# Sliding-window attention and an expert layer on one core: values' products with the exponentials as weights, tokens on partitions

## The chip, the cores and the metric

The kernel runs on one core of a Trainium2 chip. The metric is the device time of one execution in microseconds (us). A NeuronCore has a matrix engine (PE, TensorE), a vector engine (DVE), a scalar engine (ACT), a general engine (POOL, GpSimd) and a queue engine that issues transfers (SP). Matrix products are written to PSUM, eight banks of 512 f32 columns on 128 partitions; DVE and ACT copy them to SBUF.

## What is computed

Eight batches with eight heads of 576 tokens and 64 channels go through attention in which a token sees itself and the 127 tokens before it, with a slope by head. The result, 4608 tokens of 512 channels, goes to a layer of eight experts: each token to the expert with the highest logit.

```
scores = q k^T / 8;  mask = (0 <= i - j < 128)
attn = softmax(where(mask, scores - slope[h] * |i - j|, -1e9));  x = attn v     # then (B*S, H*D) = (4608, 512)
logits = x w_gate;  e = argmax(logits);  g = softmax(logits)[e]
y = g * (relu(x w1[e]) w2[e])
```

## The kernel before

**Attention.** The work is cut into 16 units: four pairs of batches (`bp`) times four pairs of heads (`hp`, 128 channels). In a unit, `c` is the batch of the pair and `r` the head of the pair. Keys are cut into nine blocks `kb` of 64 tokens; a block of keys meets at most 192 queries. Four groups `g` of a unit hold the key blocks (0,1), (2,3), (4,5), (6,7,8). `scores(i)` makes the scores of group `i` with keys on partitions (L739), one exponential over both heads (ACT, L745) and one multiplication by a table of slopes and mask (DVE, L748 or L753). The result `pe` has keys on partitions (batch `c` on its half) and queries along the free dimension. Scores run two groups ahead (`AHEAD = 2`).

`values(u, half, kbs)` has `v` (64 keys x 64 channels) as weights and `pe` (64 keys x up to 192 queries) as the moving operand. Its result has channels on partitions and queries along the free dimension, in the two banks of `at` (pool `ps_a`, one buffer of two banks), once for queries 0 to 319 and once for 320 to 575. `finish` copies `at` to `xT` (ACT, L791 and L793) and makes the sums of the exponentials with a second set of products (L806): an indicator `ind` as weights, `pe` as the moving operand once more, into a bank `m` of pool `ps_m` (two buffers); DVE adds them to `sumT` (L817), ACT copies the first (L815).

**Routing.** When a pair of batches is through, `behind(bp)` gives a list of tasks, of which `some()` runs one entry after each group: `gate` (three products of `xT` with the gate's weights, L826), `turn` (transposes of the logits and sums so that tokens are on partitions, L850), `scale_a` to `scale_c` (reciprocals of the sums, logits, softmax, on DVE), `count`, `place`, `ones_at`, `enlist` (each token's slot at its expert), and nine rows: `row_turned` transposes 128 tokens of `xT` (L984) and copies them (ACT, L986), `row_out` adds the scales (POOL, L990) and writes the row tile to `x_d` (SP, L992). After the third pair of batches the list is dense (ten entries) and ends with a gather (L1090, POOL) of the first expert's tokens. The last pair's tasks run inside the first expert group (`with_tail`).

**Experts.** For each expert four tiles of 128 tokens are gathered, scaled (L501), transposed (L1107), and multiplied in a Strassen form (L1273, L1330), with single tiles (L1369, L1385) for what exceeds 512 tokens. This part begins at 195.16 us and fills the rest.

**Order.** All of it has a manual schedule: an engine runs its instructions in the order in which the program emits them, and waits where an operand or a buffer is late. On PE the order in a step is scores of two groups on, values of this group, then one entry of tasks. On ACT the exponential of two groups on stands ahead of the copies of this group, and on DVE its multiplication does. SP issues the loads of `q`, `k` and half of `v` two units ahead (three buffers each), the row tiles and the expert weights; POOL the other half of `v`, and the gathers.

An f32 matrix product is two passes on PE, each with its own weight load; a transpose is one. With weights of 64 rows and 64 columns four products lie at four places of the array: rows by `c`, columns by `r`.

## Time and profile before

Times of three runs: 717.45, 714.87 and 713.62 us, median 714.87. The profiled execution took 721.67 us, its span is 719.9 us, the mean granted PE clock 0.987.

| what | value |
| --- | --- |
| busy share of the span | PE 95%, DVE 48%, ACT 31%, POOL 18% |
| attention and most of routing | to 195.16 us, where the first expert product starts |
| first expert group with the last pair's routing | 195.16 us to 259.73 us, where the second one's products start |
| first exponential of units 3, 7 and 11 | 37.28, 75.86 and 120.21 us |
| products of values, of sums, of scores (instructions, passes) | 1408, 704, 1152 |
| bytes moved | 122.00 MB, mean 169 GB/s |

A busy share of PE is of little use as a bound, since ends of matrix instructions are modelled and overlap. What one step costs is read from the starts of successive groups in the timeline.

### The profile page before, as it was taken

How to read it: one execution, taken by the hardware profiler on the slowest of the kernel's cores; microseconds unless marked ns; L12 is line 12 of the kernel's file. 1: busy time of each engine (PE TensorE's matmuls, PEld its weight loads, DVE VectorE, ACT ScalarE, POOL GpSimd, SP SyncE). 2: the span in 40 equal slices, each digit the busy share in tenths (PEclk: the TensorE clock that was granted, in tenths of full speed). 3: DMA queues.
4: the chain of work that ended last, by engine and by line, in shares of the span. 5: the costliest groups of instructions: out<-in, count | busy, mean ns of one | idle time of the engine just before them, and what ended most of it. 6: DMA issues, size and time to landing. Idle time of an engine off the chain costs nothing.

```text
span 719.9 us, 14588 instructions
## 1 busy us (share of the span) xinstructions
PE 683.4 (95%) x6204; PEld 570.3 (79%) x6204; DVE 347.1 (48%) x671; ACT 225.5 (31%) x410; POOL 132.1 (18%) x222
## 2 busy tenths in 40 slices
PE   6799999889899999999999999999999999999995
PEld 5677778667678888878887888788788978878892
DVE  3356738775457675443642545255245534433410
ACT  4455546455334223202311321232133023203200
POOL 4320133310200250023022102301220230021020
PEclk9999999999999999999999999999999999999998
DMA  9977876773424961186328236731843482184010
GB/s 249 241 208 264 235 229 182 194 211 109 126 76 166 354 244 45 74 272 226 117 81 305 111 117 199 293 117 27 287 182 117 164 303 77 64 287 153 1 59 8
DMA packets 52091, 122.00 MB, mean 169 GB/s; under 512 B 3679, under 2 KB 14527, under 8 KB 52016
## 3 DMA queue, kind: packets, MB, share of 16 engines
q1 hardware_dynamic: 43120, 95.66, 40.0%
q0 software_dynamic: 7744, 24.43, 10.2%
q8 instruction: 51, 0.84, 0.5%
q10 hardware_dynamic: 1152, 0.88, 0.4%
q14 instruction: 24, 0.20, 0.1%
HBM read 101.79 MB, written 19.96 MB: 169 GB/s over the span
## 4 chain that ended last, share of the span: by engine, by line
issue 57%; PE 22%; POOL 10%; DVE 4%; ACT 3%; DMA 3%; POOLq 0%; SPq 0%; ACTq 0%; DVEq 0%
PE sp L739 6%; PE at L774 6%; POOL out_dram L1353 5%; POOL xg L1090 5%; PE m L984 2%; PE m L806 2%; DMA q_sb<-in_qT_dram 2%; ACT pe L745 1%; PE m L970 1%; PE pair0b L1273 1%; ACT xT L791 1%; PE m L826 1%; DVE pe L748 1%; DMA out_dram<-zo,s_idx 1%; PE m L850 1%
## 5 line engine op out<-in xcount | busy, mean ns | idle before, releaser
L1353 POOL DMA_INDIRECT out_dram<-zo,s_idx x39 | 43.8, 1123 | 384.2 <-DVE zo L1344 283.4
L748 DVE TENSOR_TENSOR pe<-pe,fac 128x768 f32<-128x768 f32 x48 | 48.3, 1007 | 48.7 <-ACT pe L745 48.6
L774 PE MATMUL at<-pe,v_sb 64*64 64x192 f32 (+2 forms) x1408 | 63.0, 292 | 9.1 <-ACT xT L791 6.5
L739 PE MATMUL sp<-q_sb,k_sb 64*64 64x192 f32 (+2 forms) x1152 | 61.7, 330 | 7.5 <-DMA q_sb<-in_qT_dram 6.5
L745 ACT ACTIVATE pe<-sp 128x768 f32<-128x768 f32 x64 | 51.9, 810 | 51.2 <-PE sp L739 45.5
L774 PEld LDWEIGHTS at<-pe,v_sb 64*64 64x64 f32 x1408 | 48.5, 138 | 15.6 <-ACT xT L791 8.6
L739 PEld LDWEIGHTS sp<-q_sb,k_sb 64*64 64x64 f32 x1152 | 42.8, 141 | 19.8 <-issue 6.4
L1090 POOL DMA_INDIRECT xg<-x_rows,g_idx x39 | 42.7, 1094 | 30.6 <-DVE tb L1013 13.2
L806 PE MATMUL m<-pe,ind 128*32 128x192 f32 (+2 forms) x704 | 30.4, 288 | 5.3 <-issue 4.9
L1108 ACT COPY xgT<-m 128x512 f32<-128x512 f32 x39 | 22.8, 585 | 36.8 <-PE m L1107 35.9
L1284 ACT ACTIVATE h<-h 128x512 f32<-128x512 f32 x32 | 20.2, 630 | 40.3 <-DVE h L1283 35.0
L986 ACT COPY xs<-m 128x512 f32<-128x512 f32 x36 | 20.5, 584 | 33.1 <-PE m L984 23.9
L806 PEld LDWEIGHTS m<-pe,ind 128*32 128x32 f32 x704 | 23.4, 110 | 8.3 <-issue 5.8
L501 DVE TENSOR_TENSOR xn<-xg 128x512 f32<-128x512 f32 x39 | 26.1, 685 | 7.6 <-PE m L1107 6.6
L990 POOL COPY xs<-ext 128x16 f32<-128x16 f32 x36 | 10.5, 303 | 85.7 <-DMA x_rows<-xs 40.1
L608 POOL DMA_DIRECT2D v_sb<-in_v_dram x15 | 11.2, 744 | 77.4 <-PE at L774 75.6
L1107 PE MATMUL m<-ident,xn 128*128 128x128 f32 x156 | 23.6, 274 | 0.7 <-DVE xn L501 0.7
L1107 PEld LDWEIGHTS m<-ident,xn 128*128 128x128 f32 x156 | 19.2, 141 | 4.9 <-PE m L1107 0.9
L984 PE MATMUL m<-ident,xT 128*128 128x128 f32 x144 | 22.5, 289 | 0.5 <-DVE hole L1021 0.5
L1385 PE MATMUL pair2a<-w,h 128*128 128x512 f32 x48 | 21.1, 592 | 0.0
L984 PEld LDWEIGHTS m<-ident,xT 128*128 128x128 f32 x144 | 16.9, 150 | 3.9 <-issue 1.7
L791 ACT COPY xT<-at 128x640 f32<-128x640 f32 (+1 forms) x32 | 18.6, 581 | 2.9 <-PE at L774 2.2
(357 smaller groups left out, 1389.8 us busy)
## 6 DMA issues: line engine op xcount, KB each, us to landing
w<-in_moe_w_dram SPq DMA_DIRECT2D x30, 2048.0 KB, 8.9
k_sb<-in_kT_dram SPq DMA_DIRECT2D x15, 576.0 KB, 6.6
q_sb<-in_qT_dram SPq DMA_DIRECT2D x15, 576.0 KB, 7.4
x_rows<-xs SPq DMA_DIRECT2D x32, 264.0 KB, 2.6
v_sb<-in_v_dram SPq DMA_DIRECT2D x15, 288.0 KB, 6.9
v_sb<-in_v_dram POOLq DMA_DIRECT2D x15, 288.0 KB
x_rows<-xs SPq DMA_DIRECT2D x8, 132.0 KB, 2.4
xg<-x_rows,g_idx POOLq DMA_INDIRECT x39
```

Source lines behind the costliest of these rows:

```text
L501: nc.vector.tensor_tensor(to.rearrange("p (h d) -> p h d", h=H), rows[:, :Dm].rearrange("p (h d) -> p h d", h=H), rows[:, Dm : Dm + H].uns ...
L739: nc.tensor.matmul(sp[c * KB : (c + 1) * KB, r, c0 : c0 + n], lhsT=k_sb[u][hs, c, kb * KB : (kb + 1) * KB], rhs=q_sb[u][hs, c, kb * KB : k ...
L745: nc.scalar.activation(pe[:], sp[:, :, :GC], AF.Exp, scale=SCALE)
L748: nc.vector.tensor_tensor(pe.rearrange("p r (k c) -> p r k c", k=2), pe.rearrange("p r (k c) -> p r k c", k=2), fac[:, h0 : h0 + 2, None, ...
L774: nc.tensor.matmul(acc[r * D : (r + 1) * D, c, lo - q0 : hi - q0], lhsT=v_sb[u][c * KB : (c + 1) * KB, kb, r * D : (r + 1) * D], rhs=pe[c ...
L791: nc.scalar.copy(xT[bp][:, hp, : 2 * LQ].rearrange("p (b q) -> p b q", b=2)[:, :, q0 : q0 + n], acc[:, :, :n])
L806: nc.tensor.matmul(sm[32 * j : 32 * j + 32, lo - q0 : hi - q0], lhsT=none[:] if pe is None else ind[:, hp, :], rhs=fac[:, 0, :KB] if pe is ...
L984: nc.tensor.transpose(ps[:, hp * P : (hp + 1) * P], xT[bp][:, hp, t * P : (t + 1) * P], ident[:])
L1090: nc.gpsimd.indirect_dma_start(out=g["xg"][:, j, :], out_offset=None, in_=src, in_offset=bass.IndirectOffsetOnAxis(ap=g_idx[:, g["c0"] + j ...
L1107: nc.tensor.transpose(tp[:, db * P : (db + 1) * P], xn[:, db * P : (db + 1) * P], ident[:])
L1108: nc.scalar.copy(g["xT"][:, :, j * P : (j + 1) * P], tp.rearrange("p (d q) -> p d q", d=DB))
L1353: ins = nc.gpsimd.indirect_dma_start(out=out[:, :], out_offset=bass.IndirectOffsetOnAxis(ap=s_idx[:, g["c0"] + j : g["c0"] + j + 1], axis= ...
```

## The change

The operands of the values' products change places. `pe` (64 keys x 64 queries) is now the weights, and `v` of one head (64 keys x 64 channels, and beside it a column of ones) the moving operand of 65 columns. The result has tokens on partitions, and the column of ones yields the sum of the exponentials. A tile of `v` has 130 columns: ones, head 0, head 1, ones. Places of the array are by `c` (rows) and by the parity of the query block (columns); a product of which only one parity is there (the first query block's step, the last block) has two places at a time.

- `values(u, g, between)` makes, in group `g`, the two query blocks `2g` and `2g+1` (in the last also block 8), each over up to three key blocks, in two banks out of three (`ps_a` has three single banks; `ps_m` is left with one during attention, and has two after it). ACT copies the bank of `c = 0` into the row tile `R`, DVE that of `c = 1`; in the last group each copies block 8 too.
- The second products (L806), their copies and additions, `finish`, `ind` and `none` are gone.
- `R[bp]` holds nine tiles of 128 tokens as they go to `x_d` (520 columns instead of 528). `to_gate` transposes a tile of `R` for the gate (nine times for a pair of batches), into `xT` of two tiles. `gate` is made five times with up to 256 tokens, copied by ACT. `turn` is made five times with two tiles; DVE takes the reciprocal of the sums and multiplies straight out of PSUM.
- `row_turned` and `row_out` are gone. `scale_c` writes the scales into the columns of sums in `R`, and `rows_out` writes the tiles in three calls (two transfers of four tiles and two of 64 rows). `token_scales` reads the new layout.
- `some()` is called at four places of a group: in the middle and at the end of the scores, in the middle and at the end of the values. The lists get more and smaller entries, in those of the first two pairs every second one empty. `within` starts nine transposes and gates in the last unit of the pair itself.
- `ones_at` makes `oc` with two instructions instead of nine; `scale_a` adds heads in three steps instead of one reduction.
- The loads of unit 2 and 3 are emitted somewhat later, in the same order on SP.

```
-                        nc.tensor.matmul(
-                            acc[r * D : (r + 1) * D, c, lo - q0 : hi - q0],
-                            lhsT=v_sb[u][c * KB : (c + 1) * KB, kb, r * D : (r + 1) * D],
-                            rhs=pe[c * KB : (c + 1) * KB, r, c0 + lo - kb * KB : c0 + hi - kb * KB],
+            acc = [ps_a.tile([P, 512], F32, name="at") for c in range(2)]
+            if g:
+                steps = [[(2 * g, 2 * g - 2 + s), (2 * g + 1, 2 * g - 1 + s)] for s in range(3)]
+            else:
+                steps = [[(0, 0), (1, 0)], [(1, 1)]]
...
+                nc.tensor.matmul(
+                    acc[c][j * KB : (j + 1) * KB, x0 + r * (D + 1) : x0 + (r + 1) * (D + 1)],
+                    lhsT=pe[c * KB : (c + 1) * KB, r, k0 : k0 + KB],
+                    rhs=v_sb[u][c * KB : (c + 1) * KB, kb, r * (D + 1) : (r + 1) * (D + 1)],
...
+            for s, step in enumerate(steps):
+                for r in range(2):
+                    for qb, kb in step:
+                        for c in range(2):
+                            product(c, qb % 2, r, qb, kb, 0)
+                if s == 0:
+                    between()
+            if g == 3:
+                for kb in range(NK - 3, NK):
+                    for r in range(2):
+                        for c in range(2):
+                            product(c, c, r, NK - 1, kb, HW)
+            xs = slice(hp * HW, (hp + 1) * HW)
+            for c, copy in enumerate((nc.scalar.copy, nc.vector.tensor_copy)):
+                copy(R[bp][:, 4 * c + g, xs], acc[c][:, :HW])
...
+        def to_gate(bp, k, part):
+            t = slice_of(k)[part]
...
+            ps = m_bank()
+            for hp in range(HP):
+                nc.tensor.transpose(
+                    ps[:, hp * P : (hp + 1) * P], R[bp][:, t, hp * HW + 1 : hp * HW + 1 + P], ident[:],
+                )
+            nc.scalar.copy(xT[bp, k][:, :, part * P : (part + 1) * P], ps.rearrange("p (h q) -> p h q", h=HP))
...
+            todo = [[T(3, 0)], [G(2)], [T(3, 1)], [U(1)], [T(4, 0)], [G(3)], [U(2)], [G(4)], [U(3)], [U(4)], [i], [a],
+                    [b], [n, c], outs[0:1], outs[1:2], outs[2:3], [p], [], [o], [], [e]]
+            return [f for t in todo for f in (t, [])]
...
+            if g == 0:
+                return [T(0, 0), [], T(0, 1), []]
+            if g == 1:
+                return [T(1, 0), G(0), T(1, 1), []]
+            return [T(2, 0), G(1), T(2, 1), U(0)]
```

In the lists T is `to_gate`, G `gate`, U `turn`, i `in_range`, a, b, c the scales, n `count`, p `place`, o `ones_at`, e `enlist`.

## Prediction

> **What bounds the kernel now.** I read the page's groups first, then the chain of waits, the table of windows, and the timeline of single steps.
>
> ```profile
> span 719.9 us, 14588 instructions
> ...
> L748 DVE TENSOR_TENSOR pe<-pe,fac 128x768 f32<-128x768 f32 x48 | 48.3, 1007 | 48.7 <-ACT pe L745 48.6
> L774 PE MATMUL at<-pe,v_sb 64*64 64x192 f32 (+2 forms) x1408 | 63.0, 292 | 9.1 <-ACT xT L791 6.5
> L739 PE MATMUL sp<-q_sb,k_sb 64*64 64x192 f32 (+2 forms) x1152 | 61.7, 330 | 7.5 <-DMA q_sb<-in_qT_dram 6.5
> L745 ACT ACTIVATE pe<-sp 128x768 f32<-128x768 f32 x64 | 51.9, 810 | 51.2 <-PE sp L739 45.5
> ...
> L806 PE MATMUL m<-pe,ind 128*32 128x192 f32 (+2 forms) x704 | 30.4, 288 | 5.3 <-issue 4.9
> ```
>
> ACT and DVE wait for PE (45.5 and 48.6 us of idle time end that way), PE hardly for them: attention is bound by PE, whose stream L806 takes 30.4 us of. The expert part is PE alone and is not changed, so everything is decided before the first expert group's end. Two rows of the chain and three of the timeline give the pace:
>
> ```profile
> 75.86 0.81 ACT pe L745
> ...
> 120.21 0.81 ACT pe L745
> ```
>
> ```profile
> 37.28 0.81 ACT L745 ACTIVATE pe<-sp 128x768 f32<-128x768 f32 x1 [0.39 <-PE sp L739]
> ...
> 38.73 0.89 PE L774 MATMUL at<-pe,v_sb 64*64 64x64 f32 x24 [0.50 <-ACT xT L791]
> ...
> 45.10 0.81 ACT L745 ACTIVATE pe<-sp 128x768 f32<-128x768 f32 x1 [0.39 <-PE sp L739]
> ...
> 195.16 1.89 PE L1273 MATMUL pair0a<-xgT,w 128*128 128x256 f32 x8
> ```
>
> Unit 3, without tasks, takes 45.10 - 37.28 = 7.82 us. Units 3 to 10, with two pairs' routing, take (120.21 - 37.28) / 2 = 41.5 us for four. From 120.21 to the first expert product are 75.0 us.
>
> **What a step costs.** The 24 passes at 38.73 are six steps of four places, of 2 x (64 + 128 + 192) = 768 columns; 0.89 less 0.22 (one pass of 64 columns alone, 229 ns by form) is 0.67 us: 0.87 ns a column, 0.056 us for a step of 64. Rows for the copies and for a task:
>
> ```profile
> 108.82 0.72 PE L774 MATMUL at<-pe,v_sb 64*64 64x192 f32 x16
> ...
> 109.48 0.66 PE L984 MATMUL m<-ident,xT 128*128 128x128 f32 x4
> ...
> 110.06 0.88 PE L739 MATMUL sp<-q_sb,k_sb 64*64 64x192 f32 x16
> ...
> 110.22 0.59 ACT L986 COPY xs<-m 128x512 f32<-128x512 f32 x1 [0.34 <-PE m L984]
> ```
>
> ```profile
> L793 ACT COPY xT<-at 128x128 f32<-128x128 f32 x16 | 4.5, 282 | 0.0
> ...
> L833 DVE TENSOR_TENSOR gs<-m,sumT 128x128 f32<-128x128 f32 x3 | 0.9, 288 | 1.9 <-PE m L826 1.9
> ...
> L975 DVE COPY listed<-m 128x48 f32<-128x48 f32 x1 | 0.2, 209 | 1.7 <-PE m L970 1.7
> ```
>
> **The change, part by part.**
>
> *A unit without tasks.* Scores stay: 3072 columns, 2.6 us. Values: 8, 12, 12 and 24 steps in the four groups (block 8 and half of the first group have two places only), 56 x 0.056 = 3.1 us, against 3072 columns before, 2.6. So the exchange alone costs 0.5 us; what it gains is L806 (1600 columns, 1.4 us, with two changes of array shape) and the wait of 0.50 for `xT`. PE 5.7 us. New waits: three banks hold one and a half groups, and ACT copies its bank only after the exponential that stands before it (0.23 from the end of PE's stream to ACT's start: a pass of 192 columns outlasts its slot by some 0.16, and 0.07 for the signal; then 0.81, the copy 0.28, 0.05 back: 1.37 us after the scores' end). The next group needs that bank after 0.44 to 1.3 us of values and 0.65 of scores: it waits 0.3 us behind the first group, some 0.05 behind two others. In all 6.1 us, 1.7 less than 7.82. ACT needs 4 x 0.81 + 5 x 0.28 = 4.6, DVE 4 x 0.96 + 5 copies. A copy of 130 columns from PSUM isn't there: above 0.21 (48 columns), under 0.48 (128x320 with an addition, L817); I take 0.29, the row of 128 columns. DVE 5.3 us.
>
> *The bank of the tasks.* `ps_m` keeps one bank in attention. A transpose of a tile holds it from 109.48 to 110.22 + 0.59 = 110.81, and 0.05 for the wake-up: 1.38 us. A gate of 256 tokens 0.43 + 0.23 + 0.37 (L815, 256 columns) + 0.05, about 1.0; a turn, with a multiplication of 0.29, 0.8. Nine, five and five are a chain of 12.4 + 5 + 4 = 21.4 us. They stand at almost every second place from the second group of a pair's last unit on, a few tenths of PE work apart, and PE can't pass a waiting task: behind it stand the rest of the scores, and so the next exponential. Exponentials get between these evictions on ACT, by the orders of both engines about every third, and the reciprocals and multiplications of `turn` stand behind a 0.96 us multiplication on DVE twice: +3. So about 24.5 us for two units; of PE work there are only 12.1 + 6.8. Bounds: 21.4 (nothing gets between) and 24.5 + 6 (every eviction behind an exponential).
>
> *The chain of small DVE instructions.* Before, 18 entries spread it over 4.5 units; now i, a, b, n, c, p, o fall into six groups of the next two units. By the rows of before (0.17 to 0.42 each, `orow` 1.35, `oc` twice 0.56 from 1.35 x 432/1152 with 0.05) and the copies, DVE needs 9.9 us in the one and 2.9 + 3.7 in two groups of the next, where PE has 6.1 and 2.9. Scores run only two groups ahead, and the bank of `c = 1` comes free only behind all of it, so PE gives way: some 15.5 us, then two groups with `enlist` (2.0) 5.5: 21. With it, four units cost 24.5 + 21 = 45.5.
>
> *Changes of array shape.* From 64x64 to 128x128: the 16 passes at 108.82 stream 4 x 0.135 = 0.54, yet the transposes start 0.66 later, 0.12 lost; four transposes stream 0.43 and the scores follow after 0.58. About 0.25 for a task, now 21 isolated ones, before 17, some together. Where PE waits for the bank this is hidden; without that cover 21 x 0.25 = 5.3, I take 1.5: 47 us, against 41.5. Twice: **+11**.
>
> [...]
>
> *The last stretch.* The third pair's list was ten dense entries, in which PE waited (2.3 us for `pre` at L925 alone); now it has 34 small places. Its bank phase and DVE phase as above, shorter by 2 to 4 us for want of empty places, `early_table` and the gather at the same unit: 47 us to the start of unit 15. There eight transposes of 1.4 (four of them the expert's) follow one another through the bank, 11 us, then 3 with two banks; 64 in all, against 75: **-11** (bounds -16 and 0).
>
> *The tail inside the first expert group.* Six of nine transposes, two gates and a turn have moved to unit 15: L826 and L850 and L984 take 2.6 + 1.5 + 4.0 = 8.1 us of PE's row there now, 3.3 remain, as do the waits on `place` and `enlist`: **-4.5**.
>
> *The start.* Units 1 and 2 took 22.7 us (first exponentials at 14.62 and 37.28), of which DMA, clock and instructions took part:
>
> ```profile
> 0.00:18.00 18.00, 11.00 (x212) 9.09 (x216) 7.11 (x10) 8.33 (x13) 8.01 (x37) 1.00 0.93 249
> 18.00:36.00 18.00, 13.19 (x311) 11.11 (x306) 6.67 (x8) 8.22 (x16) 6.25 (x44) 0.91 0.94 241
> ...
> 28.08 0.63 PE L806 MATMUL m<-pe,ind 128*32 128x192 f32 x13 [3.74 <-issue]
> ```
>
> A unit's loads are 1.77 MB, 7.1 us at 249 GB/s, so 6.1 can't be had while DMA is 93% busy; and PE has 384 value instructions a unit in place of 264 with the sums, so a wait such as the 3.74 may come more often. Bounds: -8 (all of the pace) and 0; I take **-4.5**. Order of loads on SP and POOL is the same, three memsets stand ahead of them on POOL (0.1 to 0.2 each by L658 and L663), hidden behind the first landing at 4.44. Row transfers are four in place of ten, POOL's row copies go (10.5 us, off the path).
>
> **Sum.** -4.5 + 11 - 11 - 4.5 = -9 us of 721.67, 1.2%. On the median, which is 1% below the profiled execution: 714.87 x 0.988 = 706.
>
> **Rivals.** (1) *The bank decides, slower.* If most evictions stand behind an exponential, the bank phase costs 30 instead of 24.5, and the tasks' changes of shape come on top (4): +9 for each pair, and +5 in unit 15. -9 + 18 + 5 = +14: 729. It decides from 51.5 us for four units on. For it: no task has a second bank to go to; against: the timeline shows ACT idle half of the time now. (2) *Waits are absorbed.* Copies at 0.21, nothing between the evictions: four units 42, the last stretch 3 better: -9 - 10 - 3 = -22, 693. (3) *Offsets cancel*: the start and the tail give nothing since DMA and instructions bound there: 0, 715. (4) *Weight loads not hidden*: a step then takes as long as four loads' busy time in L774's PEld row, 48.5 us / 352 = 0.138, 4.6 us more a unit where PE has no slack, five units: -9 + 23 = +14, 729; the step of 0.056 speaks against it.
>
> **Chances.** Forecast 0.38, (2) 0.14, (3) 0.18, (1) 0.27, (4) 0.03. A difference of 0.5% is what a measurement of this kernel can tell. Faster 0.52, same 0.18, slower 0.30. The forecast's own range is 699 to 711; for 8 in 10 it reaches to (2) and to most of (1): 690 to 728.
>
> **What would show it.** No L806; a values' step of 0.056 us; a unit without tasks at 6.1 us; in a pair's last unit PE waits for ACT `xT` and `gs` before transposes and gates, 5 to 6 us a pair; in the two next units PE's values wait for DVE's copies into `R`; four units at 47. I am wrong if four units take over 51 (bank), or the start loses more to instruction waits.

## The result, with the profile after

The changed kernel takes 750.61 us, median of four runs (747.42 to 752.64), against 715.0 us for the kernel before beside it: a ratio of 1.049, 95% interval 1.0443 to 1.0537. It is slower, where 706 us was forecast and 728 was the upper end of the range. The profiled execution took 747.42 us.

From the page of the changed kernel: the span, the first line of the engines, the granted clock by slices, and the groups of PE and DVE that the change concerns.

```profile
span 745.7 us, 16443 instructions
...
PE 687.2 (92%) x7164; PEld 570.4 (76%) x7164; DVE 351.8 (47%) x707; ACT 222.6 (30%) x442; POOL 118.4 (16%) x178
...
PEclk9999799799799899999999999999999999999998
...
L781 PE MATMUL at<-v_sb,pe 64*64 64x65 f32 x3072 | 85.0, 235 | 9.4 <-issue 4.6
...
L741 PE MATMUL sp<-q_sb,k_sb 64*64 64x192 f32 (+2 forms) x1152 | 75.5, 345 | 18.4 <-issue 10.3
...
L820 PE MATMUL m<-ident,R 128*128 128x128 f32 x144 | 23.8, 286 | 6.1 <-DVE pr L855 3.5
...
L803 DVE COPY R<-at 128x130 f32<-128x130 f32 x64 | 18.5, 289 | 16.9 <-PE at L781 16.3
```

The second products are gone, which had 30.4 us and, with the empty ones of the first group, 35.4 us of PE's busy time; but the values' row has gone from 63.0 to 85.0 us (L781), and the transposes from 17.5 to 21.8 up to the first expert product (23.8 in all, L820). The PEclk line of before is all 9 but for its last slice; here three slices of attention stand at 7 and one of the first expert group at 8.

Two tables of windows, cut at the first exponentials of units 3, 7 and 11 and at the first expert product; in the second table the cuts lie 0.42 us behind these exponentials, which start at 35.73, 84.55 and 142.03 us. First the kernel before:

```profile
core 0: us, PE busy (x) PEld busy (x) DVE busy (x) ACT busy (x) POOL busy (x), PEclk, DMA share, GB/s
...
37.28:75.86 38.58, 36.03 (x883) 29.27 (x881) 24.94 (x48) 21.41 (x38) 6.08 (x14) 1.00 0.77 239
75.86:120.21 44.35, 42.18 (x928) 33.62 (x925) 28.74 (x68) 24.84 (x43) 9.71 (x17) 1.00 0.72 219
120.21:195.16 74.95, 65.93 (x1279) 52.82 (x1276) 47.43 (x109) 35.82 (x62) 17.45 (x29) 0.95 0.53 155
```

and the changed kernel, from its first instruction to past the first expert group, with the same columns:

```profile
0.00:36.15 36.15, 22.36 (x726) 19.91 (x730) 16.17 (x28) 16.92 (x34) 11.79 (x73) 0.95 0.92 248
36.15:84.96 48.81, 39.55 (x1121) 30.24 (x1112) 26.52 (x69) 24.24 (x52) 4.93 (x12) 0.97 0.62 197
84.96:142.44 57.48, 47.47 (x1179) 36.96 (x1179) 35.95 (x82) 24.18 (x52) 10.58 (x10) 0.88 0.58 172
142.44:222.43 79.99, 65.48 (x1594) 51.66 (x1595) 46.09 (x111) 34.85 (x75) 8.68 (x9) 0.91 0.51 162
222.43:285.00 62.57, 60.92 (x311) 51.49 (x310) 39.29 (x112) 16.09 (x33) 7.10 (x7) 0.95 0.45 163
```

Units 3 to 10 go from 82.9 to 106.3 us, the stretch behind them from 75.0 to 80.4, the start from 37.28 to 35.73. By the windows of the tables, over the three stages from unit 3 to the first expert product PE's busy time is 144.1 before and 152.5 after, its idle time 157.88 - 144.14 = 13.7 before and 186.28 - 152.50 = 33.8 after. Of 28.4 us lost there (28.8 from the exponential itself), 20.0 are idle time and 8.4 are longer busy time of PE, and the column PEclk tells why it is longer: 1.00, 1.00, 0.95 before, 0.97, 0.88, 0.91 after.

The stretches of half clock themselves (windows of the changed kernel, cut at the clock's changes; the sum is of six stretches, two are shown):

```profile
77.96:81.37 3.41, 3.41 (x88) 3.41 (x82) 1.55 (x3) 1.24 (x3) 0.73 (x1) 0.50 0.85 311
88.20:95.03 6.83, 6.21 (x66) 5.83 (x70) 2.14 (x5) 0.27 (x1) 0.00 (x0) 0.50 1.04 320
...
sum 30.72, PE 28.62 PEld 26.60 DVE 18.79 ACT 7.13 POOL 1.51; mean PE 4.77 PEld 4.43 DVE 3.13 ACT 1.19 POOL 0.25
```

30.7 us at 0.50, against 6.8 in the same part of before (158.6 to 162.0, 185.9 to 189.3). PE is busy for 28.6 us of them, so at full clock the same work would have taken up to 14.3 us less (before 3.4), an estimate: half of the busy time. Even net of all of that PE's own work is hardly less: 152.5 - 14.3 = 138.2 against 144.1 - 3.4 = 140.7. The exchange took one kind of work off PE and put nearly as much of others on it. The idle time, by what ended it in the same windows: waits for instructions 2.2 us before and 9.4 after, waits for DVE and ACT 11.5 and 23.3.

What PE waited for in the whole span (us in total, times, the longest):

```profile
PE sp L741 <- issue: 10.3, 4, 4.4
...
PE m L971 <- DVE orow L961: 8.0, 4, 2.8
PE at L781 <- issue: 4.6, 3, 2.4
PE at L781 <- DVE R L803: 4.1, 3, 2.1
PE m L820 <- DVE pr L855: 3.5, 5, 0.9
PE m L923 <- DVE pre L914: 2.6, 1, 2.6
```

"issue" is waiting for nothing that the profile shows. It is 6.9 us in the kernel before and 15.1 here. DVE's small chain (`pr`, `pre`, `orow`) is 14.1 here. In the timeline, such a stop lies in the middle of the scores' products, and the clock is at half 0.7 us behind its end:

```profile
72.48 0.49 PE L741 MATMUL sp<-q_sb,k_sb 64*64 64x192 f32 x5
77.25 0.64 PE L741 MATMUL sp<-q_sb,k_sb 64*64 64x192 f32 x9 [4.28 <-issue]
77.63 2.40 PE L781 MATMUL at<-v_sb,pe 64*64 64x65 f32 x68
```

The trace's records of transfers tell what the "issue" is. One queue carries instructions in pieces of 16 KB (`q8 instruction: 58, 0.95 MB`; 51 in the kernel before). The stops of over 2 us for instructions, in this kernel and the first two experiments, lie behind products 220, 347, 728, 855, 1619 or 1747, counted from 0, which is 92 and a multiple of 127.3 to within one product. So a piece is reckoned at 127 to 128 products with their weight loads. In this kernel's three such stops PE started its last product at 21.19, 36.20 and 72.65 us, a fetch ended at 24.49, 37.54 and 75.72, and PE went on 1.3 to 1.5 us later. For the stop above:

```
                      product  time (us)
piece begun             1493    70.17
fetch of the next starts        74.69
fetch ends                      75.72
PE stops (piece used up) 1619   72.65
PE goes on                      77.25
a piece in units 3 to 15: 4.4 to 11.1 us in the kernel before, 2.7 to 10.8 in the changed one
(from its first product to that of the next, a stop at its end counted in)
```

### The profile page after: what moved, and what is told of

It is laid out like the page before. It is cut to its first block, busy times and chain, and to the rows that moved or that the text cites. A ratio compares the mean times of both kernels' runs of the same rounds, so it can differ in the third digit from the quotient of the medians.

```text
span 745.7 us, 16443 instructions
## 1 busy us (share of the span) xinstructions
PE 687.2 (92%) x7164; PEld 570.4 (76%) x7164; DVE 351.8 (47%) x707; ACT 222.6 (30%) x442; POOL 118.4 (16%) x178
## 4 chain that ended last, share of the span: by engine, by line
issue 54%; PE 23%; POOL 9%; DVE 8%; ACT 3%; DMA 2%; POOLq 0%; SPq 0%; DVEq 0%
PE at L781 6%; PE sp L741 5%; POOL out_dram L1362 5%; POOL xg L1084 4%; PE m L820 3%; DMA q_sb<-in_qT_dram 2%; PE m L971 2%; DVE pe L752 2%; ACT pe L749 2%; PE pair0b L1282 1%; DVE pe L757 1%; PE m L829 1%; PE pair1a L1339 1%; PE pair0a L1282 1%; PE pair1b L1339 1%
## 5 line engine op out<-in xcount | busy, mean ns | idle before, releaser
L781 PE MATMUL at<-v_sb,pe 64*64 64x65 f32 x3072 | 85.0, 235 | 9.4 <-issue 4.6
L781 PEld LDWEIGHTS at<-v_sb,pe 64*64 64x64 f32 x3072 | 76.8, 147 | 22.0 <-issue 13.4
L741 PE MATMUL sp<-q_sb,k_sb 64*64 64x192 f32 (+2 forms) x1152 | 75.5, 345 | 18.4 <-issue 10.3
L752 DVE TENSOR_TENSOR pe<-pe,fac 128x768 f32<-128x768 f32 x48 | 49.7, 1036 | 51.8 <-ACT pe L749 51.8
L741 PEld LDWEIGHTS sp<-q_sb,k_sb 64*64 64x64 f32 x1152 | 45.5, 147 | 26.2 <-issue 18.9
L820 PE MATMUL m<-ident,R 128*128 128x128 f32 x144 | 23.8, 286 | 6.1 <-DVE pr L855 3.5
L803 ACT COPY R<-at 128x130 f32<-128x130 f32 x64 | 17.1, 267 | 39.7 <-PE at L781 39.1
L823 ACT COPY xT<-m 128x512 f32<-128x512 f32 x36 | 21.1, 587 | 25.4 <-PE m L820 25.3
L820 PEld LDWEIGHTS m<-ident,R 128*128 128x128 f32 x144 | 15.4, 140 | 14.7 <-DVE pr L855 5.5
L803 DVE COPY R<-at 128x130 f32<-128x130 f32 x64 | 18.5, 289 | 16.9 <-PE at L781 16.3
L1101 PE MATMUL m<-ident,xn 128*128 128x128 f32 x156 | 23.6, 274 | 1.8 <-ACT xT L823 1.0
L1101 PEld LDWEIGHTS m<-ident,xn 128*128 128x128 f32 x156 | 19.1, 141 | 6.2 <-ACT xT L823 2.4
L757 DVE TENSOR_TENSOR pe<-pe,fac 128x768 f32<-128x768 f32 x16 | 15.3, 954 | 12.0 <-ACT pe L749 12.0
L971 PE MATMUL m<-oc,orow 128*128 128x48 f32 x72 | 12.3, 341 | 8.0 <-DVE orow L961 8.0
```

The lines of the kernel that those rows point to most:

```text
L741: nc.tensor.matmul(sp[c * KB : (c + 1) * KB, r, c0 : c0 + n], lhsT=k_sb[u][hs, c, kb * KB : (kb + 1) * KB], rhs=q_sb[u][hs, c, kb * KB : k ...
L752: nc.vector.tensor_tensor(pe.rearrange("p r (k c) -> p r k c", k=2), pe.rearrange("p r (k c) -> p r k c", k=2), fac[:, h0 : h0 + 2, None, ...
L781: nc.tensor.matmul(acc[c][j * KB : (j + 1) * KB, x0 + r * (D + 1) : x0 + (r + 1) * (D + 1)], lhsT=pe[c * KB : (c + 1) * KB, r, k0 : k0 + K ...
L803: copy(R[bp][:, 4 * c + g, xs], acc[c][:, :HW])
L820: nc.tensor.transpose(ps[:, hp * P : (hp + 1) * P], R[bp][:, t, hp * HW + 1 : hp * HW + 1 + P], ident[:],)
L971: nc.tensor.matmul(ps[:, : E * NS], lhsT=orow[:, t, :], rhs=oc[:, t, :], start=(t == 0), stop=(t == TPB - 1),)
```

## The experiments

Twelve variants of the changed kernel stand in one table; four of the kernel before follow with their question. Instruction waits are sums of PE's waits for "issue", eviction waits those for DVE and ACT, and half clock is the sum of its stretches before the end; all are of the profiled execution.

```
kernel                            median   ratio [interval]        instr  evict  half clock
before                            715.0                              6.9   14.1   13.7
changed                           750.61   1.049 [1.044, 1.054]     15.1   24.9   41.0
tasks at two places               751.70   1.050 [1.042, 1.057]     13.0   28.4   64.9
first w1 load in four             751.81   1.050 [1.043, 1.057]     14.4   26.2   54.6
spare transposes at enlist        747.02   1.045 [1.038, 1.052]     16.6   16.7   27.3
copies of values on ACT           748.24   1.045 [1.038, 1.052]     15.1   24.3   51.2
first w1 load late                749.42   1.047 [1.038, 1.057]     14.0   26.8   51.2
enlist, place later               746.63   1.042 [1.039, 1.046]     20.9   20.4   37.5
the same, copies on ACT           745.79   1.044 [1.041, 1.046]     23.5   13.7   37.5
two banks for tasks               744.22   1.041 [1.038, 1.044]     11.5   27.0   34.1
two banks, copies on ACT          738.67   1.031 [1.024, 1.038]     14.7   16.5   44.4
the same, enlist, place later     739.65   1.031 [1.023, 1.038]     29.0    3.5   44.4
loads of a unit spread            750.29   1.048 [1.041, 1.055]     13.5   27.0   44.4
the last two, and w1 late         745.61   1.041 [1.033, 1.049]     27.7   10.9   41.0
```

And the lengths of units 3 to 10, from first exponential to first exponential, us:

```
unit                3      4      5      6      7      8      9     10    3-6    7-10
before            7.82  10.13  10.49  10.13  10.12  14.55  10.49   9.20   38.6   44.4
changed          11.28  16.31   8.67  12.55  17.59  16.11   8.67  15.12   48.8   57.5
two places       12.23  13.27  12.03  12.01  17.78  13.02  12.57  11.82   49.5   55.2
two banks        11.07  13.77  10.09  12.51  15.59  14.18  11.73  15.11   47.4   56.6
two banks, ACT   12.89  13.62   8.64  13.03  17.71  13.62   8.64  11.55   48.2   51.5
```

### Is it the packing of the tasks, and their one bank?

The lists of the first two pairs without their empty entries, and at two places of a group instead of four:

```diff
-            return [f for t in todo for f in (t, [])]
+            return todo
...
-                scores(i + AHEAD, some)
+                scores(i + AHEAD, some if u >= 11 else None)
...
-            values(u, g, some)
+            values(u, g, some if u >= 11 else (lambda: None))
```

> Tasks of the first two pairs at two places of a group instead of four, without empty entries, so that 31 entries cover nearly four units; the third and fourth pair as in the changed kernel. If the loss is the packing of the tasks (one bank in one pair of units, DVE's small instructions in the next, PE idle and then at half clock), units 3 to 6 and 7 to 10 take 43 to 46 us each (48.8 and 57.5 in the changed kernel), and the time falls by 10 to 18 us, to 733 to 741. If it is the exchange of the operands itself (more passes, more instructions to fetch), both stay above 48 and the time stays within 5 us of 751.

It brought nothing: 751.7. Units 4 and 8, the dense ones, fall by 3 us, units 5 and 9 rise by 3.4 to 3.9. Standing alone, each task pays its change of array shape: by the starts of products, a transpose's four take 0.59 in place of 0.43 and the product ahead of them 0.12 to 0.17 more. The changed kernel has the same 0.59. So a task costs about 0.3 us of PE in both, near the 0.25 that the prediction had taken, of which it then counted only 1.5 us for 21 tasks.

Two banks for tasks and two for values instead of one and three:

```diff
-        ps_m = [pool(fast, "ps_m", 1, space=PSUM)]
+        ps_m = [pool(fast, "ps_m", 1, space=PSUM), pool(fast, "ps_m1", 1, space=PSUM)]
...
-        ps_a = pool(att, "ps_a", 3, space=PSUM)
+        ps_a = pool(att, "ps_a", 2, space=PSUM)
```

> The changed kernel with two banks for the tasks and two in place of three for the values' products. Theory of the prediction 'the tasks' one bank paces a pair's last unit and the one behind it': units 4 and 8, 16.3 and 16.1 now with full clock in both, come down to 13 to 14 as in the kernel with the tasks spread, while each of the 64 groups waits for the copies of the one before (0.3 to 0.8 us, 12 units without dense tasks: 12 to 30 us in all): 750 to 775. Rival 'the bank does not pace, PE's own work does': units 4 and 8 stay at 15 or more, the time is 765 to 785.

Units 4 and 8 come down to 13.8 and 14.2, as the theory of the one bank said, so that bank costs some 2 us in each. The price in the other groups, set at 12 to 30 us, came (18.9 us more of waits for DVE's copies, below), but PE's other waits for DVE and ACT went from 20.8 to 4.0 us at the same time, which the sum had not: 744.2, 6 us under the changed kernel. What waited for the bank now waits for DVE's copies of the values:

```profile
PE at L781 <- DVE R L803: 23.0, 20, 3.2
```

23.0 us, against 4.1 in the changed kernel. The copies stand behind DVE's small chain.

### Is it DVE?

Both copies of the values on ACT:

```diff
-            for c, copy in enumerate((nc.scalar.copy, nc.vector.tensor_copy)):
+            for c, copy in enumerate((nc.scalar.copy, nc.scalar.copy)):
```

> Both copies of a group's values are made by ACT; DVE makes none. If DVE is what holds PE in the two units after a pair (its copies stand behind its small instructions and hold banks), units 5 and 6 and units 9 and 10 get 2 to 5 us shorter each pair, and the time falls by 4 to 10 us. If the bank of the tasks decides, ACT's eviction chain grows by up to 0.27 us a group and the time is the same or up to 6 us longer.

748.2, 2.4 us under the changed kernel, where more was expected; its runs (747.6 to 748.7) lie within those of the changed kernel (747.4 to 752.6), so that no gain is shown. Then the tasks in which PE stands longest for DVE, given more time (the third pair's list likewise):

```diff
-                    [b], [n, c], outs[0:1], outs[1:2], outs[2:3], [p], [], [o], [], [e]]
+                    [b], [n, c], outs[0:1], outs[1:2], outs[2:3], [p], [], [o], [], [], [], [], [e]]
```

> The changed kernel, with enlist three places later in the first two pairs' lists and place and enlist two and five places later in the third's, so that DVE has orow and pre done when PE comes to them. Theory 'PE waits for DVE's chain because it is given too little time, and each wait halves the clock behind it': the gaps of 3.05 (85.78), 2.36 (142.11), 1.79 (189.61) and 2.93 (181.24) shrink or go with the half clock behind them (88.2 to 95.0, 146.2 to 149.6, 183.8 to 190.6, 194.0 to 197.4): 5 to 12 us less, 739 to 745. Rival 'PE has to wait for DVE anyway, there or at the values' copies': 748 to 752.

> The same places, and both copies of the values on ACT in place of one on DVE, which takes 80 copies of 0.29 out of DVE's queue ahead of the chain. If DVE's lateness is what is left, 2 to 5 us less than with the places alone (734 to 743); if the values' bank now waits for ACT's exponentials, no gain over it.

746.6 and 745.8, both above what the theory of DVE's lateness said. The waits did go, in the second from 24.9 to 13.7 us; but those for instructions rose from 15.1 to 20.9 and 23.5. That is the first sign of what the last runs show plainly.

### What does the clock cost?

Spare transposes ahead of the products in `enlist`, where PE waits for `orow`:

```diff
+            for t in range(24):
+                nc.tensor.transpose(ps[:, :P], ident[:], ident[:])
```

> 24 spare transposes of the identity stand ahead of the products of enlist, in the bank that these write next; they keep PE at work for 2.6 us where it waits for the one-hot rows from DVE, and add 2.6 us where it does not wait. If the half clock comes from PE's idleness, the half-clock stretches after the four enlists (10 to 17 us of them) get shorter and the time falls by 2 to 7 us, to 743 to 748. If the clock follows something else, the time rises by 0 to 4 us.

747.0: with work that is of no use the median is 3.6 us lower, though the runs touch (746.5 to 749.3 against 747.4 to 752.6), and the half clock fell from 41.0 to 27.3 us. To price the half clock by itself, stalls were put into the kernel before, in units 3 to 7. A short stall is a transpose, ACT's copy, an addition on POOL, and a transpose for which PE waits:

```diff
+            ps = ps_m.tile([P, 512], F32, name="m")
+            nc.tensor.transpose(ps[:, :P], ident[:], ident[:])
+            nc.scalar.copy(held[:, 0, :P], ps[:, :P])
+            for k in range(1):
+                nc.gpsimd.tensor_tensor(held[:, 1 - k % 2, :P], held[:, k % 2, :P], held[:, k % 2, :P], op=ALU.add)
+            ps = ps_m.tile([P, 512], F32, name="m")
+            nc.tensor.transpose(ps[:, :P], held[:, 1, :P], ident[:])
...
+            if 3 <= u < 8:
+                stall()
```

In the kernel with half as many stalls the condition is `3 <= u < 8 and g % 2`, and there are two wide additions in place of one narrow one.

> The kernel before, with 20 stalls of PE put into units 3 to 7 (one behind each group): a transpose into a bank of the tasks, ACT's copy of it, one addition of 128x128 on POOL, and a transpose of that, for which PE waits. Nothing else is changed. A stall should be 1.2 us (0.23 from PE to ACT, copy 0.28, some 0.35 for the addition by the 1.27 of 128x512 on POOL, signals) to 2.0 (behind an exponential), 24 to 40 us in all. Theory 'the granted clock falls after long idle stretches of PE': stalls of this length leave the clock at 1.00 in units 3 to 8, and the time is 715 plus the stalls' sum, less what waits of before they cover. Rival 'the clock falls with PE's idle share, however it is cut': half clock appears here as in the kernel with half as many stalls of twice the length.

> The kernel before, with 10 stalls of PE in units 3 to 7 (behind the second and fourth group), each with two additions of 128x384 on POOL (some 0.95 each by the 1.27 of 128x512): 2.8 to 3.5 us a stall, 28 to 35 us in all, about the idle time of the 20 short ones. Theory 'the granted clock falls after long idle stretches': most of these stalls are followed by a stretch of 3.4 us at 0.50, each of which costs up to 1.7 us beyond the stall itself, so 10 to 17 us more than the stalls' sum. Rival 'idle time costs itself alone': the time is 715 plus the stalls' sum and the clock stays at 1.00.

Windows of two stages and the sum of units 3 to 8, first with 20 short stalls:

```profile
54.50:72.50 18.00, 13.68 (x261) 9.04 (x254) 6.36 (x9) 6.84 (x16) 2.36 (x5) 1.00 0.32 99
...
90.50:108.50 18.00, 11.71 (x230) 9.00 (x230) 7.38 (x20) 6.59 (x14) 3.02 (x10) 1.00 0.24 83
...
sum 100.10, PE 72.69 PEld 53.12 DVE 41.40 ACT 38.17 POOL 20.96; mean PE 14.54 PEld 10.62 DVE 8.28 ACT 7.63 POOL 4.19
```

then with 10 long ones (same columns):

```profile
54.20:72.20 18.00, 13.52 (x252) 9.20 (x248) 5.81 (x9) 6.05 (x12) 4.01 (x5) 0.91 0.34 101
...
90.20:108.20 18.00, 11.71 (x159) 8.61 (x158) 6.03 (x14) 4.77 (x9) 4.71 (x10) 0.72 0.25 80
...
sum 106.60, PE 78.96 PEld 59.15 DVE 41.87 ACT 36.06 POOL 27.95; mean PE 13.16 PEld 9.86 DVE 6.98 ACT 6.01 POOL 4.66
```

The 20 short gaps, from the start of one transpose to that of the next, are 30.1 us in all (nineteen of 1.21 to 2.04 and one of 3.02), the 10 long ones 27.6 (2.55 to 3.28). Units 3 to 8 take 100.1 us with the short and 106.6 with the long, 63.2 without any. The clock stays at 1.00 through the short stalls but for one stretch; with the long ones there are eight stretches of 3.4 or 6.8 us at 0.50. Busy time of PE rises from 72.7 to 79.0 for the same products, and to this the shorter idle time and the ten fewer stalls (with some 0.3 us of products and array changes each) are to be added: 6.5 + 2.5 + 3 = 12 us for ten long stops, an estimate of about 1.2 us each beyond the stop itself. The medians are 753.3 and 758.1. The theory holds; the rival that a wait costs only itself falls, and so does the one that the share of idle time decides however it is cut.

In the traces of the two kernels the stretches ahead of the last start multiples of 3.41 us apart: at 28.88, 158.58, 185.89 and 230.26 us in the one before, at 26.76, 77.96, 88.20, 135.98, 146.22, 183.77, 194.01 and 252.04 in the changed one. The length of a gap, from start to start, does not decide by itself: in the changed kernel one of 2.03 us, from 249.41, was followed by half clock from 252.04 on, and one of 2.60 us, from 36.20, by none until 77.96. What decides was not shown.

Then the same remedy for the kernel before, 18 spare transposes ahead of late tasks' products (`place` of the last two pairs, shown, and `enlist` of the last):

```diff
             ps = ps_m.tile([P, 512], F32, name="m")
+            if bp >= 2:
+                for t in range(18):
+                    nc.tensor.transpose(ps[:, :P], ident[:], ident[:])
```

> The kernel before, with 18 spare transposes ahead of the third and fourth pair's product in place (PE waits 2.3 us there for the third) and ahead of the fourth pair's products in enlist (1.77 idle at 226). The half clock of before stands behind such gaps: 158.6 to 162.0 behind 155.62, 230.3 to 233.7 behind 226.06. Theory 'the clock follows the idle share of a window': both stretches go, up to 1.7 us each where PE is busy; 18 transposes at 0.11 are 2.0 us, within the waits they fill, though the fourth pair's place, where nothing waited long, loses up to 2: 711 to 715 against 715, at best half a per cent under before. Rival 'the spare work costs what it takes': 717 to 721.

719.05 against 715.49, a ratio of 1.0047 (1.0029 to 1.0065). The three stretches of half clock behind 155 us are gone (a new one stands at 68.7), yet the time is longer, as the rival said: in this kernel, where waits are few, filling them is no gain.

### Where do instructions come late?

> The kernel before, with two lumps of 512 PE products of one column each (64x64, four places in turn), one behind the third group of unit 6, where the DMA share is 1.02 and the next 10 us are 0.65, and one behind the last group of attention, where it is about 0.20. Theory 'PE's instructions come in blocks of 128 products (16 KB on the instruction queue), each asked for when the one before it is begun': PE stops after every 127 to 128 products for want of instructions, a lump is paced by the fetch (about 2.5 to 4 us a block in the quiet place, where a fetch takes 0.9 to 1.4 of it, and longer in the busy one), 10 to 16 us for the quiet lump and 14 to 28 for the busy one, though the products themselves need some 20 ns each, 10 us. Rival 'instructions come as fast as PE takes them': both lumps take 7 to 11 us without a stop.

A lump is 512 products of one column in a row. It stands in the kernel before, twice:

```diff
+            for k in range(512):
+                c, j = k // 2 % 2, k % 2
+                nc.tensor.matmul(
+                    ps[c][j * KB : (j + 1) * KB, :1], lhsT=ident[c * KB : (c + 1) * KB, :KB],
+                    rhs=ident[c * KB : (c + 1) * KB, c : c + 1], start=(c, j) not in begun, stop=True,
...
```

The timeline of the quiet lump, behind attention:

```profile
217.32 2.73 PE L1171 MATMUL m<-ident 64*64 64x1 f32 x172 [0.43 <-ACT xgT L1108]
224.00 3.59 PE L1171 MATMUL m<-ident 64*64 64x1 f32 x128 [3.95 <-issue]
228.00 3.59 PE L1171 MATMUL m<-ident 64*64 64x1 f32 x128 [0.41 <-issue]
232.00 7.32 PE L1171 MATMUL m<-ident 64*64 64x1 f32 x256 [0.41 <-issue]
239.73 0.50 PE L1171 MATMUL m<-ident 64*64 64x1 f32 x13 [0.41 <-issue]
```

128 products, a stop, 128 products, a stop: from 224.00 to 228.00 to 232.00 a piece of instructions takes 4.00 us, with a DMA share of 0.33 falling to 0.01. There the products themselves take 26.5 ns at half clock (14.8 at full clock in the first piece), 3.4 us for 128. In the traces of the two kernels a fetch takes 0.88 to 1.58 us. So the theory holds for the blocks of 128 and the stops behind them; that each is asked for when the one before it is begun was not shown. The quiet lump took 23 us where 10 to 16 had been said, with one stop of 3.95 us and with half clock through all but its first piece, which had not been thought of. The other lump took 18 us and was no test of busy queues: the share of DMA had fallen to 0.08 by then.

Here the changed kernel loses what a price per column can't show. Ahead of the first expert product stand 4603 products instead of 3617; a unit has 264 (72 of scores, 192 of values) in place of 208 (72, 88, and 48 of sums). At 4.0 us for 128, 264 would take 8.25 us. That is an estimate from one stretch at half clock and no bound: in attention of the changed kernel a fetch starts 0 to 4.6 us after PE has begun on a piece (behind the first two fetches), and some pieces pass in under 4 us (the shortest in 2.7, from 200.53). But ahead of the first expert product the closest two fetches start 3.85 us apart in the trace of before and 3.38 in that of the changed kernel, and the 6.1 us of the prediction for a unit ask for a piece every 2.9 us. So that pace is held for a piece or so: from 69.49 to 72.65 us 151 products start at 21 ns each, and then comes the stop of 4.3 us.

Are fetches late because of other loads? The load of the first `w1` in four parts over units 4 to 7, the same load in unit 12, and a unit's loads spread over its groups:

```diff
-                if u == 5:
-                    load_w1(fixed[0], w1_a)
+                if 4 <= u < 8:
+                    load_w1_part(fixed[0], w1_a, u - 4)
```

> The first expert's first weights (2 MB) are loaded in four parts, one a unit from unit 4 to 7, instead of at once at unit 5. If the 4.6 us in which PE waits for instructions at 72.65 us come from that load, the wait and the half clock that follows it (77.96 to 81.37 us) go, and the time falls by 5 to 7 us, to 744 to 746. If PE simply runs out of instructions for their number, a wait of that size stays there or elsewhere and the time is 748 to 753.

```diff
-                if u == 5:
+                if u == 12:
                     load_w1(fixed[0], w1_a)
...
-            if 8 <= u < 12 and g % 2 == 1:
+            if u >= 14:
                 ws_tasks.pop(0)()
```

> The changed kernel, but the first expert's w1 is loaded at unit 12 instead of unit 5, and its sums are made in units 14 and 15. Theory 'fetches of instructions come late behind the loads': the wait of 4.3 us for instructions at 72.65, where DMA was busy 92%, goes, and with it the half clock of 77.96 to 81.37: 4 to 6 us less, 744 to 747. Rival 'the fetch is late whatever DMA carries' (as the load in four parts left 3.1 us of the same wait): 749 to 752. If the sums are late for the first expert group, it starts later than 222 and eats the gain.

```diff
-                load_unit(u + 2)
+                if g == 0:
+                    load_k(u + 2, 0, S, nc.sync)
+                elif g == 1:
+                    load_q(u + 2, 0, S, nc.sync)
+                elif g == 2:
+                    load_v(u + 2, 0, nc.sync)
+                else:
+                    load_v(u + 2, 1, nc.gpsimd)
```

> The changed kernel with a unit's loads spread: keys at its first group, queries at the second, values at the third and fourth, from unit 2 on, instead of all at the first. Theory 'fetches wait behind bursts of loads': the stops of 2.4 us at 38.8 and 4.3 at 77.25 shrink by half or more and the half clock behind the second goes; waits for instructions 15.1 us in all now, 8 to 12 then; 743 to 748. Rival 'a block of 128 products is taken faster than any fetch': no change, 749 to 753.

751.8, 749.4 and 750.3: none differs from the changed kernel. From product to product, the stop at product 1619 stays in the first (3.4 us), in the second it shrinks from 4.6 to 1.9 and others grow, in the third it is gone (1.7 one piece earlier), with its half clock, and the sum of instruction waits is still 13.5. While the first loads run, fetches start up to 7.0 us behind the beginning of a piece (16.41 to 23.39 us; 18.28 to 25.07 in the kernel before), and 4.5 at 70; that the loads of the later units cause their delay is not shown by any of the three.

### All together

Two banks for tasks, both copies on ACT; then `place` and `enlist` later; then loads spread and `w1` late.

> The changed kernel with two banks for the tasks, two for the values, and both copies of the values on ACT. Theory 'waits for evictions and DVE hold it': the 22.3 us of waits for DVE's copies become waits for ACT of 5 to 10 us, with less half clock: 730 to 738. Rival 'PE's number of products and their instructions hold it': the waits for instructions grow (6 us with two banks alone, 19 with later places and copies on ACT) as those for copies go, and the time stays at 738 to 746.

> The same with place and enlist later, as in the kernels before. By the first theory another 2 to 4 us less (727 to 735), by the rival 737 to 745, with instruction waits of 10 to 20 us between 30 and 222 us.

> Two banks for the tasks, copies on ACT, later place and enlist, the loads spread and w1 of the first expert loaded at unit 12. By the first theory the waits for instructions fall from 29 us to 15 or less, with half clock behind them: 725 to 733. By the rival they stay above 22 us: 736 to 742.

738.7, 739.7 and 745.6. PE's longest waits in the first:

```profile
PE m L971 <- DVE orow L961: 13.1, 4, 4.5
PE sp L741 <- issue: 10.7, 4, 4.4
...
PE at L781 <- issue: 4.0, 2, 2.5
```

and in the second:

```profile
PE at L781 <- issue: 14.3, 6, 4.4
PE sp L741 <- issue: 13.9, 5, 4.4
```

From the first to the second, eviction waits fall from 16.5 to 3.5 us and instruction waits rise from 14.7 to 29.0: 31.2 and 32.5 in sum, at the same half clock (44.4) and the same time. PE, held less by DVE, ran into the end of its instructions. The rival named for these runs, number of products and their instructions, holds for the first two. The third lies above both ranges (725 to 733 and 736 to 742): its instruction waits stayed at 27.7 us, as the rival said, and PE waits 6.2 us for DVE at the first expert's transposes (L1101); why it is 6 us longer was not followed up. No edit brings the changed kernel below the one before; the best is 3.1% above it.

## Why the prediction was wrong, step by step

In the profiled spans, -9 us were forecast and +25.8 came. By its steps: the start -1.6 for -4.5, units 3 to 10 +23.4 for +11, the last stretch +5.4 for -11, the tail -1.9 for -4.5. A further 10 us of the miss of the median are the base: the profiled execution of before was 1% above its median, that of the changed kernel 0.4% below.

- **What a step costs.** Right as far as it went. A values' step has a median of 0.060 us for the 0.056 forecast, the copies are 0.289 (DVE) and 0.267 (ACT) for 0.29 and 0.28. The rival of weight loads that are not hidden had 0.138 a step, and falls.
- **PE's stream outside the start.** This is the step that failed. The sum takes instructions as always at hand and the clock as full, so that a wait costs its own length alone, and counts 1.5 of 5.3 us a pair for the changes of array shape. It saw that 384 value instructions (192 products with their loads) stand in place of 264 and put that down to the start only; nothing asked how fast they can be brought. From unit 3 to the first expert product the runs show 9.4 us of waits for instructions (2.2 before) and 30.7 us at half clock (6.8 before), worth up to 10.9 us. PE's own work fell by 2.5 us, where the sum has 1.4 - 0.5 = 0.9 a unit, some 12 in 13 units; that changes of shape, at 0.3 a task, took the rest is argued and not shown.
- **A unit without tasks, 7.82 to 6.1 us.** Behind the start no unit of the changed kernel is without tasks, so this was not measured by itself. The lightest units, 5 and 9, take 8.67, with five tasks in each and PE at work throughout. The window of unit 5:

```profile
63.30:72.00 8.70, 8.69 (x301) 6.71 (x297) 5.60 (x16) 4.93 (x12) 0.74 (x1) 1.00 0.43 122
```

  By the starts of products the five tasks take 1.9 us and the products ahead of them some 0.7 more, which leaves about 6.1 (an estimate). So the columns were priced rightly, for as long as instructions were there.
- **The bank, 24.5 with 1.5 for shapes, and DVE's chain, 21.** The first pair gives 11.28 + 16.31 = 27.6 and 8.67 + 12.55 = 21.2 us, close to forecast, and in part by luck: in units 3 and 4 PE is busy for 23.1 us, where 18.9 were forecast, and waits 1.7 for DVE and ACT, where 5.6 were; in units 5 and 6 no wait of PE for DVE is listed, only the stop for instructions. Stops for instructions of 2.4 and 4.3 us are in these lengths, which were not in the sum, so the bank was overrated by 1 us and the chain by about 4. The second pair gives 33.7 and 23.8: in it lie some 13 us of half clock, a wait of 2.8 us for `orow`, and waits of 4.1 us for DVE's copies. Of the signs of being wrong, four units over 51, the second pair (57.5) gave one and the first (48.8) none. That 3.4 to 6.8 us of products at half clock came behind such waits (77.96 to 81.37 behind one of 4.28 us, 252.04 to 258.86 behind one of 1.65) was in no term; the profile had it in view, as 13.7 us of PEclk 0.5 behind gaps such as that of 2.54 us at 155.62.
- **The last stretch, 75 to 64.** It took 80.4, the largest miss of the four. Its waits for DVE's chain and for evictions are some 12 us (7.5 before), where the smaller places were to take off those of the dense list, and some 14 us are at half clock, 6.8 before. That the two phases are "shorter for want of empty places" was an argument without a row.
- **The start.** The wait for instructions that was named as a threat is there (4.4 us in place of 3.7, and one of 1.3); PE had less to do and waited longer, 13.8 us of idle time for 11.8. The bound of no gain was nearer than the -4.5.
- **The tail.** 62.7 for 64.6: right in sign, under half in size. One wait for `orow`, 1.7 us, is left with 6.8 us of half clock behind it.
- **Rivals.** "The bank decides, slower" had the right side and the wrong mechanism as the main one: two banks are worth 6 us of 36. "Waits are absorbed" fell with the first eviction waits. "Offsets cancel" was near for the start and the tail, and said nothing of the rest. Missing was the rival that took place: more products, fetched in pieces of 127 to 128, with waits of up to 4.3 us and 30.7 us of half clock.

What stays open: what sets the delay of a fetch, and how much of the 30.7 us of half clock belongs to each kind of wait. By the stall pair a stop costs about 1.2 us in it; in all, full clock could save at most 14.3 - 3.4 = 10.9 us (both estimates) from unit 3 to the first expert product.

## What to carry to other kernels

Count instructions beside columns: where an exchange of operands cuts the same products into more and shorter ones, ask whether the fetch of instructions keeps up, by the 16 KB pieces on the instruction queue in the trace (here one for 127 to 128 products), before pricing them by columns. Price a wait of PE with the half clock behind it (here an estimated 1.2 us for each long stop), and try several short waits in place of a long one: 20 stops of 30.1 us in all gave 753.3 us, 10 of 27.6 gave 758.1. When removing a wait leaves the time as it was, add up the waits by kind in both profiles: here evictions gave 13 us and instructions took 14.

## What was not expected of the hardware

- Stops for instructions came 127 to 128 products apart or a multiple of that (behind products 347, 728 and 1619 of the changed kernel). In the quiet lump 128 products took 4.00 us twice and 256 took 7.73, where 128 products themselves take 3.4. Ahead of the first expert product the closest two fetches start 3.85 us apart in the kernel before and 3.38 in the changed one.
- Stretches of half clock ahead of the last are 3.41 or 6.83 us in the traces of the two kernels, and start multiples of 3.41 us apart in each. They came behind single gaps of 2.03 us (249.41, changed kernel) to 4.60 (72.65), and behind one of 1.77 us in the kernel before (226.06), with products of 48 columns behind it. 512 products of one column, with no wait of over 0.85 us between them, led to 30.7 us of half clock as well (81.2 to 111.9, where the lump ends at 96).
- With four places of the array in turn, products of one column started every 14.8 ns at full clock and 26.5 ns at half (means of the quiet lump).
